# HGRN2 linear attention with a bilinear feed-forward layer: the states' part of a unit moved to the next unit's state sums, and the first two units rearranged

## The chip, the cores and the metric

The kernel runs on one core of a Trainium2 chip. The metric is the device time of one execution in microseconds; for each kernel several executions are timed and their median is given. A profile is one further execution, recorded by the hardware profiler. In it PE is the engine of the matrix products, DVE and ACT the two engines that work on whole tiles (vector and scalar engine), POOL the third of that kind, and SP the engine that here only issues DMAs.

## What is computed

Attention with a decaying state, for 4 batches, 8 heads, 768 tokens and 48 channels a head, and then a bilinear feed-forward layer on 3072 tokens of 384 channels, with 1536 inner channels. All inputs of the attention are fp32; the three weight matrices come as fp64.

```python
def _attn_ref(q, k, v, f_logit):
    f = 1.0 / (1.0 + np.exp(-f_logit))
    state = np.zeros((B, H, D, D), dtype=np.float32)
    for t in range(S):
        state = f[:, :, t, :, None] * state + np.einsum('bhd,bhe->bhde', k[:, :, t], v[:, :, t])
        y[:, :, t] = np.einsum('bhd,bhde->bhe', q[:, :, t], state)

def _moe_ref(x, w_a, w_b, w_out):
    a = x @ w_a
    b = x @ w_b
    return (a * b @ w_out).astype(np.float32)

# x is y with heads and channels of a token side by side: (B, H, S, D) -> (B*S, H*D)
```

## The kernel before

**Tiling.** `by_quotients` (L79) cuts the attention into 16 units. A unit `u` is one batch, one half of the sequence (`BLK` = 384 tokens) and four of the eight heads; two units after each other give all heads of one half, and so one block of 384 tokens of the feed-forward layer's input, `xT[blk]`, of which there are 8. Four heads lie in a tile of 128 partitions as two pairs: 48 rows of a head at partition 0, 48 of the next at partition 64, and the pairs side by side in the free dimension (`n`). `FIRST` are the units 0 and 1.

**The steps of a unit.** The decay's running products are divided into k and multiplied into q, and then everything is matrix products on 64-token pieces (`SUB`), of which a unit has 6 along the tokens:

- `load_unit` (L134) issues a unit's loads on SP. There are three sets of input tiles, so unit `u + 3` takes the place of unit `u`.
- `front` (L254), in four parts: sigmoids on ACT (L261 to L264), a scale on POOL (L266); scans on DVE (L271) and the test of whether the decay fits (`held`, L272); reciprocal and scans on DVE (L276, L281); products q and k (L283, L284).
- `scores` (L311): q times k on PE (L319), masked by DVE into `at` (L335).
- `turn` (L339): k transposed on PE (L347, products of 128 rows), copied into `kT` by ACT (L349, L351).
- `gains` (L355): what each piece adds to the state, kT times v on PE (L367, 24 products, 64 rows by 48 columns); then DVE adds these up along the tokens into `st`, one copy (L381) and five additions (L383), and scales the last for the next half (L390).
- `within` (L392): `at` times v (L401), into the PSUM banks of y.
- `across` (L410): state times q (L422), added into the same banks. Three copies, or four where two spare banks are used, bring y to SBUF (L435, into one tile `y` of a pool with one buffer; for the first two units ACT does those of the one bank and DVE those of the other), five small DMAs put its rows into `xT` (L450; for the first two units three on ACT's queue and two on SP's, later all on SP's), and then unit `u + 3` is loaded.

L319, L367, L401 and L422 are products on 64-row parts of PE's array: four of them, on the four quadrants, run side by side. All others use 128 rows. The profile has two records for each fp32 `matmul` of the code, so the 24 products of `gains` show as x48.

**The feed-forward layer.** `up` (L463) makes one 128-channel column of `x @ w_b` and of `x @ w_a` (L469, 12 records), `product` (L478) multiplies both (ACT copy L484, DVE L486). That is done so for the first two blocks, while the weights come in. The later blocks take `up_pair` (L528) with fewer, combined products, and `down` (L593) makes the output for two groups of 128 tokens. The weights come in pieces of 384 or 768 KB: `load_weights` (L175) issues the next piece on SP, and `from_double` (L191) makes fp32 of it in three parts, two on ACT (L202, L204, with a POOL operation; L207, L209) and one on DVE (L214, L216). `begin(n)` (L219) and `end(n)` (L230) run the first two parts and the last part of all pieces up to `n`; from the third piece on, two of them excepted, `end` also issues the load of a further piece.

**The order.** The program's order is written by hand (`tc.manual_schedule`). Each engine works through its own list in that order, and waits for the others by semaphores. Up to `up(0, 4)` the calls stand one by one (L701 to L801). From there a loop walks over `up`, `up_pair` and `down`, and between their parts `beside()` takes parts of units from a queue with due times. A unit's parts there are those of the generator `slot` (L652):

```python
def slot(u):
    nxt = front(u + 1) if u + 1 < NU else iter(())
    next(nxt, None)
    yield
    if u > 2 * NQ:
        within(u - 1)
    if u < NU:
        scores(u)
    next(nxt, None)
    yield
    if u < NU:
        turn(u)
    if u > 2 * NQ:
        across(u - 1)
    yield
    if u < NU:
        gains(u)
```

So the slot of unit `u` runs, in its second part, `within` of the unit before and `scores` of its own, in its third `turn` and `across` of the unit before, in its fourth `gains`. Between two parts stand products of the feed-forward layer, or none where both have the same due time.

## Time and profile before

| | us |
|---|---|
| median of 14 runs | 630.1 (628.55 to 631.92) |
| the profiled execution | 629.11 |
| its span, first to last instruction | 627.4 |
| PE busy in it | 593.7 |
| DVE, ACT, POOL busy | 377.7, 221.9, 62.8 |

The mean clock granted to PE was 0.984 of full speed. The page's busy times are sums over the span; the span has two very different stretches, and its slices and windows show them. Up to about 45 us units 0 and 1 go through all their steps and the first weight pieces arrive: 43.65 MB of DMA traffic in the whole span, with 185 to 255 GB/s in the first seven of 40 slices. After that PE works on the feed-forward layer, with units 2 to 15 in between.

What the head looks like, step by step, from the timelines of PE, DVE and ACT (start in us):

| step | unit 0 | unit 1 |
|---|---|---|
| k landed | 13.09 | |
| scores (L319) | 15.55 | 23.84 |
| mask (L335) | 18.32 | 25.93 |
| within (L401) | 19.35 | 26.59 |
| gains (L367) | 20.63 | 28.12 |
| states on DVE (L381, L383) | 21.90 | 29.55 |
| across (L422) | 23.25 | 29.86 |
| first copy of y (L435) | 24.25 | 33.20 |
| first DMA into xT (L450) | 25.35 | 33.84 |
| first products of block 0 (L469) | 32.03 | |

### The profile page before, as it was taken

The numbers are of one execution on the slowest core, as the hardware profiler recorded it, in microseconds if no ns is written. First come the engines' busy times: TensorE is split into PE (matmuls) and PEld (weight loads), VectorE is DVE, ScalarE is ACT, GpSimd is POOL, SyncE is SP. The second block draws the span as 40 slices with busy tenths as digits, with TensorE's granted clock in tenths as the row PEclk, the third lists the DMA queues.
The fourth block names the chain that finished last, engine by engine and source line by source line (L and its number), as shares of the span: only waits on it lengthen the run. The fifth ranks groups of instructions, "written<-read, shape, count | busy, mean of one in ns | idle before, by whom it ended". The sixth has DMA issues, their size and how long they took to land.

```text
span 627.4 us, 13968 instructions
## 1 busy us (share of the span) xinstructions
PE 593.7 (95%) x5922; PEld 537.1 (86%) x5922; DVE 377.7 (60%) x748; ACT 221.9 (35%) x400; POOL 62.8 (10%) x58
## 2 busy tenths in 40 slices
PE   0869899999999999999999999999999999999996
PEld 0736555558998999999999999999999999999995
DVE  6877445797877567646675567647564344534541
ACT  6578499722332243224312242323311232022200
POOL 6234154410000000000000000000000000000000
PEclk9869999999999999999999999999999999999998
DMA  8786775000144304130404012040001000000000
GB/s 235 222 254 192 189 248 187 1 1 1 46 108 115 96 7 90 41 83 1 96 1 120 27 32 65 11 111 2 20 1 46 26 19 2 2 27 0 1 26 30
DMA packets 30343, 43.65 MB, mean 70 GB/s; under 512 B 3776, under 2 KB 24896, under 8 KB 30272
## 3 DMA queue, kind: packets, MB, share of 16 engines
q1 hardware_dynamic: 29984, 42.38, 24.8%
q8 instruction: 48, 0.79, 0.6%
q10 hardware_dynamic: 288, 0.30, 0.2%
q14 instruction: 23, 0.19, 0.1%
HBM read 33.23 MB, written 4.72 MB: 60 GB/s over the span
## 4 chain that ended last, share of the span: by engine, by line
PE 87%; DMA 5%; DVE 2%; SPq 2%; ACT 1%; issue 1%; ACTq 0%; DVEq 0%
PE ps_f L542 41%; PE ps_f L610 23%; PE ps_f L469 14%; DMA xT<-y 2%; PE ps_y L401 2%; PE ps_x L319 2%; PE ps_x L367 2%; PE ps_y L422 1%; PE ps_x L347 1%; DMA v_in<-in_v_dram 1%; SPq L154 1%; SPq L450 1%; DMA out_dram<-o 1%; DMA k_in<-in_k_dram 1%; DMA q_in<-in_q_dram 1%
## 5 line engine op out<-in xcount | busy, mean ns | idle before, releaser
L542 PE MATMUL ps_f<-xT,w_ba 128*128 128x192 f32 x864 | 155.4, 327 | 0.0
L547 DVE TENSOR_TENSOR groups<-ps_f,groups 128x384 f32<-128x384 f32 x144 | 80.1, 558 | 118.5 <-ACT groups L559 99.5
L542 PEld LDWEIGHTS ps_f<-xT,w_ba 128*128 128x128 f32 x864 | 142.3, 190 | 0.5
L469 PE MATMUL ps_f<-xT,w_ba 128*128 128x384 f32 x288 | 98.2, 501 | 5.7 <-DVE w_ba L216 4.2
L469 PEld LDWEIGHTS ps_f<-xT,w_ba 128*128 128x128 f32 x288 | 55.2, 194 | 46.1 <-DVE w_ba L216 5.8
L542 PE MATMUL ps_f<-b_sb,raw 128*128 128x192 f32 x432 | 82.0, 326 | 0.0
L542 PEld LDWEIGHTS ps_f<-b_sb,raw 128*128 128x128 f32 x432 | 72.2, 190 | 0.0
L550 ACT COPY groups<-ps_f 128x384 f32<-128x384 f32 x36 | 17.3, 480 | 109.3 <-PE ps_f L542 103.6
L610 PE MATMUL ps_f<-w_out,h 128*128 128x192 f32 x288 | 52.0, 330 | 0.6 <-DVE o L605 0.6
L610 PE MATMUL ps_f<-w_out,groups 128*128 128x192 f32 x288 | 50.9, 327 | 0.0
L610 PE MATMUL ps_f<-spare,h 128*128 128x192 f32 x288 | 49.6, 328 | 0.2 <-DVE h L605 0.2
L610 PEld LDWEIGHTS ps_f<-w_out,h 128*128 128x128 f32 x288 | 46.8, 190 | 1.6 <-DVE o L605 0.9
L610 PEld LDWEIGHTS ps_f<-w_out,groups 128*128 128x128 f32 x288 | 47.3, 190 | 0.1
L610 PEld LDWEIGHTS ps_f<-spare,h 128*128 128x128 f32 x288 | 46.8, 190 | 0.8 <-issue 0.5
L205 POOL TENSOR_SCALAR h<-h 128x768 f32<-128x768 f32 (+1 forms) x20 | 40.6, 2028 | 49.4 <-ACT h L202 47.5
L266 POOL TENSOR_SCALAR inv<-inv 128x768 f32<-128x768 f32 x14 | 13.5, 962 | 306.2 <-ACT inv L262 306.2
L605 DVE TENSOR_TENSOR o<-ps_f,u 128x192 f32<-128x192 f32 x36 | 12.8, 355 | 44.0 <-PE ps_f L610 40.7
L572 DVE TENSOR_TENSOR groups<-groups 128x384 f32<-128x384 f32 x72 | 36.6, 549 | 0.0
L559 ACT COPY groups<-ps_f 128x384 f32<-128x384 f32 x36 | 17.3, 480 | 52.6 <-PE ps_f L542 52.6
L542 PE MATMUL ps_f<-xT,raw 128*128 128x192 f32 x144 | 29.8, 330 | 0.0
L542 PE MATMUL ps_f<-b_sb,w_ba 128*128 128x192 f32 x144 | 29.3, 326 | 0.0
L319 PE MATMUL ps_x<-q_in,k_in 48*64 48x64 f32 x672 | 13.7, 226 | 16.3 <-DVE start L276 15.6
(113 smaller groups left out, 700.6 us busy)
## 6 DMA issues: line engine op xcount, KB each, us to landing
q_in<-in_q_dram SPq DMA_DIRECT2D x32, 144.0 KB, 4.1
k_in<-in_k_dram SPq DMA_DIRECT2D x32, 144.0 KB, 3.5
v_in<-in_v_dram SPq DMA_DIRECT2D x16, 288.0 KB, 5.0
raw<-in_moe_w_out_dram SPq DMA_DIRECT2D x6, 768.0 KB, 4.3
out_dram<-o SPq DMA_DIRECT2D x24, 192.0 KB, 1.9
f_in<-in_f_logit_dram SPq DMA_DIRECT2D x28, 144.0 KB, 3.0
xT<-y SPq DMA_DIRECT2D x46, 72.0 KB, 2.2
raw<-in_moe_w_b_dram SPq DMA_DIRECT2D x4, 768.0 KB, 7.1
```

The source lines that it names most:

```text
L205: nc.gpsimd.tensor_scalar(h, h, HI_MAX, None, ALU.min)
L266: nc.gpsimd.tensor_scalar(inv, inv, EXP_K, 1.0, ALU.mult, ALU.add)
L319: nc.tensor.matmul(ps[h][SUB * p:SUB * p + SUB, o:o + SUB], lhsT=kf[r, tokens(n, c, p)], rhs=qf[r, tokens(n, c, p)], start=True, stop=True,)
L367: nc.tensor.matmul(ps_x[R * h:R * h + D, p, (n * NC + c) * D:(n * NC + c) * D + D], lhsT=kT[r, n, c, R * h:R * h + D], rhs=t["v"][r, n, c, ...
L469: nc.tensor.matmul(ps[nm][:, 0:BLK], lhsT=w[:, kt, ft * 128:ft * 128 + 128], rhs=x[:, kt], start=kt == 0, stop=kt == NKT - 1,)
L542: nc.tensor.matmul(to[:, g], lhsT=w[:, g, j], rhs=x, start=start and g == 0, stop=True, skip_group_check=True)
L547: nc.vector.tensor_tensor(c[:, :, k, i], x, y, ALU.add)
L550: nc.scalar.copy(p1, x0)
L559: nc.scalar.copy(u3, x0)
L572: nc.vector.tensor_tensor(to[:, :, 2 * j + k], a[:, :, k], b[:, :, k], ALU.mult)
L605: nc.vector.tensor_tensor(to, x, y, op)
L610: nc.tensor.matmul(to, lhsT=x[:, i], rhs=w[:, i], start=first and i == 0, stop=i == HFT - 1, skip_group_check=True)
```

## The change

Three things are done at once.

1. In `slot` one `yield` moves up: `across(u - 1)` leaves the part of `turn(u)` and stands at the head of the part of `gains(u)`.
2. For units 0 and 1: `y` lies in a slice of `groups` of its own for each unit rather than in the pool's one tile; all five DMAs into `xT` go on ACT's queue; unit 0's copies of y are all on ACT; `gains` sums the state up inside PSUM, with 48 products instead of 24, then one ACT copy and three DVE operations in place of one copy and five additions; the test `held` and the scaling for the next half move out into `check` and `carry`, which are called later.
3. The calls of the head are put into another order: unit 0's loads stand ahead of unit 1's, the first three weight pieces ahead of k of unit 0, `across(0)` behind `scores(1)` and `turn(1)`, `end(4)` (which begins and ends the fourth weight piece) ahead of `across(1)`, `turn(2)` ahead of `within(2)`.

```diff
--- before.py
+++ after.py
@@ -251,6 +251,10 @@
     def halves(x):
         return x.rearrange("p n s -> p (n s)")
 
+    def check(u):
+
+        nc.vector.tensor_tensor(held[:, u], products_of_f[u][:, :, BLK - 1], least, ALU.is_ge)
+
     def front(u):
 
         t = sets[u % NSET]
@@ -269,7 +273,8 @@
         for n in range(2):
             c = slice(n * BLK, n * BLK + BLK)
             nc.vector.tensor_tensor_scan(F[:, c], F[:, c], none, math.exp(MIDDLE), ALU.mult, ALU.add)
-        nc.vector.tensor_tensor(held[:, u], products_of_f[u][:, :, BLK - 1], least, ALU.is_ge)
+        if u not in FIRST:
+            check(u)
         yield
 
         start = sb2.tile([128, 2, NC - 1], FP32, tag="start", name="start")
@@ -357,6 +362,7 @@
         _, half, _ = unit(u)
         t, kT = sets[u % NSET], live[u]["kT"]
         last = half == NH - 1
+        at_once = u in FIRST
         for n in range(2):
             for c in range(NC):
                 for p in range(2):
@@ -364,16 +370,26 @@
                         continue
                     for h in range(2):
                         r = slice(SUB * p, SUB * p + SUB)
-                        nc.tensor.matmul(
-                            ps_x[R * h:R * h + D, p, (n * NC + c) * D:(n * NC + c) * D + D],
-                            lhsT=kT[r, n, c, R * h:R * h + D],
-                            rhs=t["v"][r, n, c, h * D:h * D + D],
-                            start=True,
-                            stop=True,
-                        )
+                        for ci in range(0 if at_once else c, c + 1):
+                            nc.tensor.matmul(
+                                ps_x[R * h:R * h + D, p, (n * NC + c) * D:(n * NC + c) * D + D],
+                                lhsT=kT[r, n, ci, R * h:R * h + D],
+                                rhs=t["v"][r, n, ci, h * D:h * D + D],
+                                start=ci == 0 or not at_once,
+                                stop=ci == c,
+                            )
         st = sb3.tile([128, NJ, 2, D], FP32, tag="st", name="st")
         before = live[u - NQ]["st"][NJ] if half else None
         live[u]["st"] = [before] + [st[:, j] for j in range(NJ - 1 if last else NJ)]
+        if at_once:
+
+            sums = [ps_x[:, p, 0:2 * NC * D].rearrange("r (n c d) -> r c n d", n=2, c=NC) for p in range(2)]
+            even, odd = (st.rearrange("r (c p) n d -> r p c n d", p=2)[:, p] for p in range(2))
+            nc.scalar.copy(odd, sums[1])
+            nc.vector.tensor_copy(even[:, 0], sums[0][:, 0])
+            nc.vector.tensor_tensor(even[:, 1:], sums[0][:, 1:], odd[:, 0:NC - 1], ALU.add)
+            nc.vector.tensor_tensor(odd, sums[0], odd, ALU.add)
+            return
         for j in range(NJ - 1 if last else NJ):
             c, p = divmod(j, 2)
             new = ps_x[:, p, 0:2 * NC * D].rearrange("r (n c d) -> r n c d", n=2, c=NC)[:, :, c]
@@ -382,9 +398,14 @@
             else:
                 nc.vector.tensor_tensor(st[:, j], before, new, ALU.add)
             before = st[:, j]
-        before = live[u]["st"][-1]
-        if not last:
-
+        carry(u)
+
+    def carry(u):
+
+        if u in FIRST:
+            check(u)
+        if unit(u)[1] < NH - 1:
+            before = live[u]["st"][-1]
             for n in range(2):
                 end = products_of_f[u][:, n, BLK - 1:BLK]
                 nc.vector.tensor_scalar(before[:, n], before[:, n], end, math.exp(-MIDDLE), ALU.mult, ALU.mult)
@@ -427,11 +448,15 @@
                         stop=True,
                         skip_group_check=True,
                     )
-        y = sb1.tile([128, 2 * NC, 2, SUB], FP32, tag="y", name="y")
+        if u in FIRST:
+
+            y = groups[:, NTG, u * 2 * BLK:u * 2 * BLK + 2 * BLK].rearrange("r (o p m) -> r o p m", p=2, m=SUB)
+        else:
+            y = sb1.tile([128, 2 * NC, 2, SUB], FP32, tag="y", name="y")
 
         whole = [(0, 0, 0, 128)] if ps[0] is y_banks[0] else [(0, 0, 0, D), (0, R, R, D)]
         for p, e, r, rows in (*whole, (1, R, 0, D), (1, 0, R, D)):
-            copy = nc.vector.tensor_copy if u in FIRST and p else nc.scalar.copy
+            copy = nc.vector.tensor_copy if u == 1 and p else nc.scalar.copy
             copy(y[r:r + rows, :, p], ps[p][e:e + rows, 0:BLK].rearrange("r (o m) -> r o m", m=SUB))
         give_back(ps)
         y = y.rearrange("r (n c) p m -> r n (c p m)", n=2)
@@ -446,7 +471,7 @@
                     kt, p = divmod(ch, 128)
                     w = min(left, 128 - p)
 
-                    queue = nc.scalar if u < NQ and (n + h) % 2 else nc.sync
+                    queue = nc.scalar if u in FIRST else nc.sync
                     queue.dma_start(out=xT[blk][p:p + w, kt], in_=y[row:row + w, n])
                     ch, row, left = ch + w, row + w, left - w
         live.pop(u - NQ, None)
@@ -662,9 +687,9 @@
         yield
         if u < NU:
             turn(u)
+        yield
         if u > 2 * NQ:
             across(u - 1)
-        yield
         if u < NU:
             gains(u)
         yield
@@ -713,92 +738,93 @@
 
         load_unit(0, "f")
         load_unit(1, "f")
+        patterns()
+        load_weights()
+        load_weights()
+        next(fronts[0])
+        load_unit(0, "q")
+        load_weights()
+        next(fronts[1])
+        next(fronts[0])
+        load_unit(2, "f")
+        load_unit(0, "k")
+        next(fronts[1])
+        load_unit(0, "v")
         next(fronts[0])
         load_unit(1, "q")
-        load_unit(0, "q")
-        load_unit(1, "k")
-        load_weights()
-        load_unit(0, "k")
-        load_weights()
-        patterns()
         next(fronts[0])
-        load_weights()
-        next(fronts[0])
-        load_unit(1, "v")
-        next(fronts[1])
-        next(fronts[1])
-        next(fronts[0])
-        load_unit(0, "v")
         next(fronts[1])
         begin(3)
-        load_unit(2, "k")
-        load_unit(2, "f")
         scores(0)
-        load_unit(2, "v")
+        load_unit(1, "v")
+        turn(0, True)
+        load_unit(1, "k")
         next(fronts[1])
-        turn(0, True)
         within(0)
         gains(0)
+        next(fronts[2])
+        load_unit(2, "v")
+        scores(1, True)
+        load_weights()
+        turn(1, True)
+        load_unit(2, "k")
         load_unit(NSET, "f")
-        load_weights()
+        load_unit(NSET + 1, "k")
+        end(3)
+        load_unit(2, "q")
+        across(0)
         next(fronts[2])
-        turn(1, True)
-        across(0)
-        load_weights()
-        scores(1, True)
-        end(2)
         within(1, True)
-        load_unit(2, "q")
         gains(1)
+        end(4)
         across(1)
-        load_weights()
+        begin(4.5)
         next(fronts[2])
         next(fronts[3])
-        end(3)
-        next(fronts[2])
-
-
-        up(0, 0)
         next(fronts[2])
         load_unit(NSET, "q")
-        begin(4.5)
+
+
+        up(0, 0)
+        product()
+        load_unit(NSET + 1, "f")
+        load_unit(NSET, "v")
+        next(fronts[3])
+        carry(0)
+        scores(2, True)
+        up(0, 1)
+        begin(5)
+        end(6)
         load_weights()
         product()
-        load_unit(NSET, "v")
-        end(4)
-        scores(2, True)
-        up(0, 1)
-        next(fronts[3])
-        load_unit(NSET + 1, "q")
-        end(5)
-        load_unit(NSET, "k")
-        end(6)
+        turn(2, True)
         within(2)
-        load_unit(NSET + 1, "f")
-        load_unit(NSET + 1, "k")
-        turn(2, True)
         load_weights()
         gains(2)
-        load_unit(NSET + 1, "v")
+        up(0, 2)
+        load_unit(NSET, "k")
+        begin(7)
         next(fronts[3])
+        load_weights()
         next(fronts[3])
         product()
-        begin(7)
-        up(0, 2)
-        product()
         across(2)
+        begin(8)
         up(0, 3)
-        begin(8)
         scores(3)
         turn(3, True)
+        load_weights()
+        carry(1)
         within(3)
+        load_unit(NSET + 1, "q")
         gains(3)
         across(3)
-        up(0, 4)
         end(7)
         product()
+        load_unit(NSET + 1, "v")
+        up(0, 4)
+        end(8)
         product()
-        end(8)
```

## The prediction

> **What bounds the kernel now.** I read the page first, then a table of windows, PE's waits, the chain of waits, and last the timeline of PE around one unit.
>
> ```profile
> PE   0869899999999999999999999999999999999996
> PEclk9869999999999999999999999999999999999998
> ```
> ```profile
> 27.00:40.50 13.50, 7.96 (x138) 5.19 (x139) 10.68 (x25) 5.06 (x8) 2.44 (x2) 0.50 0.70 206
> 74.00:624.00 550.00, 545.56 (x5097) 504.59 (x5095) 325.46 (x642) 176.67 (x331) 35.53 (x24) 1.00 0.19 50
> ```
>
> The columns of the windows are stretch, its length, busy time and count of PE, weight load, DVE, ACT, POOL, then granted clock, DMA share and GB/s. From 74 to 624 us PE is busy for 545.56 of 550 us at full clock: there the time is the length of PE's own list of products, and only what shortens this list counts. Before that PE waits, and at 27 to 40.5 us its clock is 0.50, so the head is a chain of other engines' work:
>
> ```profile
> PE ps_x L319 <- DVE start L276: 15.6, 1, 15.6
> PE ps_f L469 <- DVE w_ba L216: 4.2, 1, 4.2
> ```
> ```profile
> 27.27 5.83 DMA xT<-y
> ...
> 35.64 4.72 DMA xT<-y
> ...
> 40.50 4.49 PE ps_f L469 x8
> ```
> ```profile
> 33.20 0.97 ACT L435 COPY y<-ps_f 48x384 f32<-48x384 f32 x2 [8.46 <-DMA xT<-y]
> ```
>
> The chain goes: y of unit 0 copied, its last small DMA into xT lands at 27.27 + 5.83 = 33.10; the one y buffer comes free, y of unit 1 is copied at 33.2 (ACT had stood idle for 8.46 us before this copy), its DMAs go out until 35.64, the last lands 4.72 us later, and the first block's products go on at 40.50. Two parts are thus to be judged: PE's list after 74 us, and the moment that stands at 40.50 here.
>
> **What the Trainium skill says.** "TensorEngine Tiling (Array Packing)", section Tiling Modes, under Key Properties: a change of the tiling mode, not of the tile alone, drains the TensorE, while tiles of one mode run independently. The trace agrees, and gives the price:
>
> ```profile
> 287.57 2.11 PE L542 MATMUL ps_f<-xT,w_ba 128*128 128x192 f32 x12
> 289.61 0.89 PE L401 MATMUL ps_y<-at,v_in 64*48 64x64 f32 x48
> 290.32 0.92 PE L319 MATMUL ps_x<-q_in,k_in 48*64 48x64 f32 x48
> 291.16 1.57 PE L542 MATMUL ps_f<-xT,w_ba 128*128 128x192 f32 x8
> ...
> 295.17 0.81 PE L542 MATMUL ps_f<-b_sb,raw 128*128 128x192 f32 x4
> 295.82 0.82 PE L347 MATMUL ps_x<-ident,k_in 128*128 128x128 f32 x6
> 296.56 0.87 PE L422 MATMUL ps_y<-q_in,st 48*48 48x64 f32 x40
> 297.37 0.92 PE L542 MATMUL ps_f<-xT,raw 128*128 128x192 f32 x4
> 298.12 2.11 PE L542 MATMUL ps_f<-xT,w_ba 128*128 128x192 f32 x12
> 300.17 0.74 PE L367 MATMUL ps_x<-v_in,kT 64*48 64x48 f32 x40
> 300.84 1.57 PE L542 MATMUL ps_f<-xT,w_ba 128*128 128x192 f32 x8
> 302.24 1.46 PE L542 MATMUL ps_f<-b_sb,raw 128*128 128x192 f32 x8
> ```
>
> Durations overlap in the pipeline, so I read differences of starts. Four full products take 0.65 us (295.17 to 295.82). Twelve should take 1.95 and take 2.05 up to the gains (298.12 to 300.17): going in costs 0.10. The eight after it take 1.40 instead of 1.30, the four after across 0.75 instead of 0.65: coming out costs 0.10. "DMA: Bandwidth & Descriptors", section "Issuing engines are not separate DMA queues": queues of several engines share the same DMA engines, so another issuer saves only its own issue time. The 4.72 and 5.83 us agree: both stood behind a 768 KB weight load that SP had issued. "TensorE: Matmul & The Clock Gate", Part 1: half rate after idling, in a window of about 3.4 us; agrees with 0.50 at 27 to 40.5 us, the clock coming back only within the next 4.5 us (mean 0.62).
>
> **Part 1: across moved from the turn to the gains.** The arithmetic is unchanged. In the new order of PE's instructions, across stands immediately ahead of gains in the 8 slots where it stood apart before: slot 5 and slots 9 to 15. In slots 6 to 8 turn, across and gains already lay next to each other, slot 4 has no across, the last no gains. In each of the 8, one way in and one way out go: 2 x 0.10 = 0.20 us by the starts above. Each batch of 64-row products also fills and empties for itself. By the single starts in the trace, its first four passes take 60 to 74 ns where later fours take 25 to 36, and from its last product to the first full one it is 135 to 146 ns, while from within to scores it is 36. That is 0.03 + 0.10, so about 0.34 us a unit, against 0.20 if these ends overlap something. I take 8 x 0.34 = **2.7 us** gained (bounds 1.6 and 2.9).
>
> What could eat it: across now comes one step later, so y, its copies (L435 on ACT), SP's xT DMAs and the next load_unit come a step later, about 3 us. Those queued behind them on SP are the loads of a unit three ahead, needed five or more steps later, and the xT of a block that has further units to wait for. The gains come no later than before, but stand behind across; their 6 adds on DVE (0.28 us each) feed the next unit's states, half a dozen steps off. The transposes are now followed at once by full products, whose inputs are old. PE is ahead of nothing here, so I cost it at nothing; if an xT came late it would cost at most the step, 3 us, once a block.
>
> **Part 2: sums at once, y tiles, queues, new head order.** From the durations above and the head's timeline:
> - Reordered loads: ahead of k of unit 0 now stand f of two units, two 384 KB weight pieces, q of unit 0, a 768 KB piece and f of unit 2, instead of 2.1 MB of f, q, k and one piece. f ended at 6.86 us; with 1.1 us for 384 KB, 1.2 for a q, k or f of a unit, 2.05 for 768 KB: 6.86 + 2.2 + 1.2 + 2.05 + 1.2 + 1.2 = 14.7, against 13.09. DVE's scans had the scores wait until 15.55, so they come at about 15.9: +0.3. The gains then start near 21.0 (before: 20.63).
> - The gains of units 0 and 1 issue 48 products each instead of 24. 24 took 1.15 us at half clock (20.63 to 21.78). Doubled: 2.0 to 2.3. On DVE one copy and five adds (0.26 + 1.40) become an ACT copy of 288 (0.4) and DVE operations of 96, 192 and 288 (about 1.1 together): 1.5 against 1.66, nearly even. Sums of unit 0 are ready near 24.8 (23.6 before), and across(0) stands behind scores(1) and turn(1), ending near 25.95 (24.2 before).
> - ACT does all three copies of y(0), behind the sigmoids of unit 2 (2.0) and the kT copies of unit 1: 26.55 to 28.0. Then it issues all five DMAs itself, 0.61 each: to 31.1. Behind these waits ACT's copy of the sums of unit 1, at 31.1; with DVE's part across(1) runs 32.0 to 34.2 (before 29.87 to 32.1).
> - Then the conversion of the fourth weight piece (`end(4)`: four ACT operations, 3.55 us with overlap) is queued ahead of the copies of y(1): 31.6 to 35.1, copies to 36.1 on ACT and, behind DVE's L214 and L216, to 37.4 on DVE. There is no wait for a buffer any more; before, these copies ran at 33.2 to 34.4. So the 8.46 us of waiting were worth only 33.2 - 32.1 = 1.1 us, and ACT's queue takes more than that back.
> - Five issues, 36.9 to 39.4, the last landing in 1.9 to 2.5 us, as no 768 KB load is ahead of it now: about 41.5. Before: 40.37.
> The moment at 40.50 goes to about 41.6: +1.1. Two switches go in the head too (within(2) now follows turn(2)), and the weight pieces come in another order, none on the path by my reckoning. Kept on to the third unit, whose xT landed at 73.09, I take **+1.3 us** for the head (bounds -0.5, where the copies of y(1) slip in front, to +5).
>
> **Sum.** -2.7 + 1.3 = -1.4 us, against the profiled execution: span 627.4, with what lies around it 629.11, to 627.7. The median of the runs, 630.1, lies 1.0 above that execution; the same difference gives **628.7 us**. A comparison of this kernel tells 0.2%, 1.26 us, from no change.
>
> **Rivals.**
> - B, slower: ACT's queue becomes the end of the head. Two groups of five issues, a copy, a conversion and y(1) stand in one line on ACT. For it: 2.12 us for three issues in the line of 25.98 us (0.71 each; single ones up to 0.83), and nothing on ACT can overtake. Against it: ACT was only 5.06 of 13.5 us busy there. Price: ten issues at 0.83 give +2.2, and one more 3.4 us window at half clock loses 1.7; 1.3 + 2.2 + 1.7 = +5.2 in the head, -2.7 after: 632.6. It decides if the DMAs of y(1) go out after 40 us.
> - C, faster: the head is neutral. The free y tile and the 3 us that DMAs no longer lose behind 768 KB loads cancel the ACT queue: 630.1 - 2.7 = 627.4; with a head 0.5 to 1.5 earlier, 626 to 627. For it: both xT waits of the chain, 5.83 and 4.72. Against it: the times worked out above.
> - D, the merging gains little: fewer crossings, but across and gains side by side wait for the four quadrants or for kT (L349, which has 0.3 and 0.2 us in PE's waits). It saves 0 to 1: with the head's 1.3, 630.4 to 631.4.
>
> **How the numbers follow.** A 0.45, B 0.20, C 0.23, D 0.12. A spreads over 627.2 to 630.2: 0.26 of it faster than the bound, 0.19 within. C: 0.20 and 0.03. B: 0.18 slower, 0.02 within. D: 0.06 within, 0.06 slower. Together faster 0.46, same 0.30, slower 0.24. The range 626.0 to 631.8 leaves out most of B (0.14) and the end of C (0.05). A alone: 627.2 to 630.2.
>
> **What would show it.** In the timeline of PE after 74 us: L422 followed directly by L367 and one late start instead of two; the stretch from there to the end shorter by 2 to 3 us. In the head: the scores of unit 0 at 15.9, no long wait ahead of L435, the last xT of unit 1 landing at 41 to 42, PE busy without gaps from a start about 1 us later. I am wrong if the products of the first block go on before 40.3 or after 43.5, or if full products after the turn wait.

## The result

| | median us | runs | ratio to before (95% interval) |
|---|---|---|---|
| before | 630.07 | 47 (628.36 to 631.92) | 1 |
| changed | 637.12 | 10 (635.16 to 641.02) | 1.0111 (1.0098 to 1.0124) |

The changed kernel is slower by 7.0 us; 628.7 was predicted, in a range of 626.0 to 631.8. Its profiled execution took 634.15 us with a span of 632.4, which is 3 us under its median, so the profile shows 5.0 of the 7 us, and what follows from it gives places rather than exact sizes.

### The profile after

First the page and the windows that answer to those of before (columns as there). From 74 us on PE is idle for 7.1 us where it was 4.4; the 2.7 us between have the length of one wait, shown below. In the head the clock of 0.81 from 27 to 40.5 us is no gain: it is 0.50 from 40.5 to 45, where it was 0.62 before.

```profile
PE   0659799999999999999999999999999999999996
PEclk9969989999999999999999999999999999999998
```
```profile
27.00:40.50 13.50, 7.52 (x237) 5.63 (x232) 9.95 (x20) 7.01 (x12) 2.13 (x1) 0.81 0.80 228
74.00:629.00 555.00, 547.87 (x5106) 506.42 (x5104) 327.17 (x645) 176.04 (x331) 35.06 (x24) 1.00 0.19 52
```

PE's waits in the changed kernel (what waits, for whom; us in total, times, longest):

```profile
PE ps_f L494 <- DMA xT<-groups: 4.5, 2, 3.9
PE ps_f L324 <- issue: 2.8, 1, 2.8
PE ps_f L494 <- DMA xT<-y: 2.7, 1, 2.7
PE ps_f L443 <- DVE st L389: 2.6, 1, 2.6
```

L494 is `up`, L324 `scores`, L443 `across`. Before's list has for `up` 4.2 us for a converted weight piece (shown above) and

```profile
PE ps_f L469 <- DMA xT<-y: 1.5, 2, 0.9
PE ps_f L401 <- issue: 1.7, 1, 1.7
```

of which 0.9 stand ahead of 40.50 and the other 0.5 ahead of 73.23; for the first state that `across` takes it waits 0.4. And the chain of waits, before (first two lines; block 0 is shown above) and after:

```profile
70.89 2.20 DMA xT<-y
73.23 72.59 PE ps_f L469 x224
```
```profile
42.09 2.19 DMA xT<-groups
...
44.38 5.07 PE ps_f L494 x8
...
72.16 6.10 DMA xT<-y
...
78.55 11.61 PE ps_f L494 x30
```

Before, the first block went on at 40.50; now it is 44.38. So 3.9 us are lost up to unit 1's transfer, and 3.7 of them are still there at across of unit 3 (69.93 against 66.19). Block 1 goes on at 78.55 where it was 73.23, after a wait of 2.7 us where it was 0.5: 2.2 us more. This wait is paid twice, since PE's clock falls after it; 4 us at a mean of 0.58 lose 1.7 us:

```profile
79.00:83.00 4.00, 4.00 (x9) 2.22 (x8) 0.00 (x0) 2.58 (x4) 1.23 (x1) 0.58 1.07 222
```

At the scores of unit 4 the changed kernel is thus 7.5 us late (153.30 against 145.75). A third, smaller loss follows there: from these scores to `within` of unit 4 it takes 17.16 us where it took 16.25, and in it PE waits for the `product` ahead (L511) once:

```profile
PE ps_f L635 <- DVE groups L511: 0.7, 1, 0.7
```

Against this stands the gain of the moved yield. The lag is +8.5 us at `within` of unit 4 (170.46 against 162.00), and then it shrinks slot by slot: at `within` of units 8, 9, 10, 11 and 15 it is +8.1, +7.7, +7.4, +6.2 and +4.8. So 3.7, 3.8 and 0.9 us are lost in three places and 3.6 gained, which leaves 4.8 of the 5.0 that the spans differ by. The slot of unit 10 in the PE timeline of the changed kernel shows how:

```profile
304.87 2.11 PE L567 MATMUL ps_f<-xT,w_ba 128*128 128x192 f32 x12
306.91 0.71 PE L443 MATMUL ps_y<-q_in,st 48*48 48x64 f32 x34
...
307.60 0.72 PE L374 MATMUL ps_x<-v_in,kT 64*48 64x48 f32 x36
308.25 1.57 PE L567 MATMUL ps_f<-xT,w_ba 128*128 128x192 f32 x8
```

Across (L443) and gains (L374) run into each other, with one way in and one way out.

### The profile page after: what moved, and what is told of

Same layout as the page of the kernel before. It is cut to its first block, busy times and chain, and to the rows that moved or that the text cites. A ratio compares the mean times of both kernels' runs of the same rounds, so it can differ in the third digit from the quotient of the medians.

```text
span 632.4 us, 14154 instructions
## 1 busy us (share of the span) xinstructions
PE 592.2 (94%) x6018; PEld 537.1 (85%) x6018; DVE 374.1 (59%) x740; ACT 223.1 (35%) x404; POOL 62.5 (10%) x58
## 4 chain that ended last, share of the span: by engine, by line
PE 87%; issue 4%; DMA 2%; DVE 2%; ACT 2%; POOL 1%; SPq 1%; ACTq 0%; DVEq 0%; POOLq 0%
PE ps_f L567 41%; PE ps_f L635 25%; PE ps_f L494 14%; PE ps_y L422 2%; PE ps_x L324 1%; PE ps_x L374 1%; PE ps_y L443 1%; POOL h L205 1%; PE ps_x L352 1%; DMA xT<-y 1%; DMA k_in<-in_k_dram 1%; DMA f_in<-in_f_logit_dram 1%; SPq L475 0%; DVE h L630 0%; ACT kT L356 0%
## 5 line engine op out<-in xcount | busy, mean ns | idle before, releaser
L494 PE MATMUL ps_f<-xT,w_ba 128*128 128x384 f32 x288 | 100.3, 509 | 7.2 <-DMA xT<-groups 4.5
L494 PEld LDWEIGHTS ps_f<-xT,w_ba 128*128 128x128 f32 x288 | 56.2, 198 | 48.6 <-DMA xT<-groups 6.7
L324 PE MATMUL ps_x<-q_in,k_in 48*64 48x64 f32 x672 | 13.7, 226 | 17.8 <-DMA q_in<-in_q_dram 17.1
```

The lines of the kernel that those rows point to most:

```text
L324: nc.tensor.matmul(ps[h][SUB * p:SUB * p + SUB, o:o + SUB], lhsT=kf[r, tokens(n, c, p)], rhs=qf[r, tokens(n, c, p)], start=True, stop=True,)
L494: nc.tensor.matmul(ps[nm][:, 0:BLK], lhsT=w[:, kt, ft * 128:ft * 128 + 128], rhs=x[:, kt], start=kt == 0, stop=kt == NKT - 1,)
```

## The experiments

Eighteen further kernels were run, each timed beside the kernel before. I name the parts of the change: S the moved yield, Y the y tiles of their own, Q ACT's queue and copies, G the sums at once, O the new order of the head. Ratios are to the kernel before of the same group of runs. The other nine come further down.

| run | parts | median us | ratio (95% interval) |
|---|---|---|---|
| e1_slot_only | S | 627.08 | 0.9956 (0.9941 to 0.9972) |
| e8_slot_and_y | S Y | 624.98 | 0.9930 (0.9912 to 0.9947) |
| e11_y_and_queue | S Y Q | 627.80 | 0.9965 (0.9953 to 0.9978) |
| e10_y_and_sums | S Y G | 628.62 | 0.9981 (0.9970 to 0.9993) |
| e3_old_order | S Y Q G | 630.74 | 1.0018 (1.0005 to 1.0030) |
| e12_order_alone | S Y O | 634.47 | 1.0072 (1.0055 to 1.0090) |
| e5_old_sums | S Y Q O | 632.02 | 1.0041 (1.0026 to 1.0057) |
| e4_split_queues | S Y G O, copies of Q | 635.61 | 1.0096 (1.0075 to 1.0118) |
| changed kernel | S Y Q G O | 637.12 | 1.0111 (1.0098 to 1.0124) |
| e2_head_only | Y Q G O | 638.20 | 1.0140 (1.0117 to 1.0164) |

### Which part costs

**e1: the yield alone.**
```diff
 # the kernel before
-        if u > 2 * NQ:
-            across(u - 1)
         yield
+        if u > 2 * NQ:
+            across(u - 1)
         if u < NU:
             gains(u)
```


> The kernel before with the one yield moved and nothing else. Theory M (merging saves about 0.34 us in each of 8 slots, the head costs the rest): 2.7 to 3.6 us faster than before, so about 627 us. Rival N (merging saves nothing, waits take its place): within 0.7 us of before, 630. Unit by unit in the trace, M expects the lead over before to grow by 0.3 to 0.4 us a slot from slot 9 to slot 15.

It is 2.8 us faster (0.44% of 630), with an interval of 1.8 to 3.7, so M holds. In the eight slots that lost a crossing the lead grows by 0.32 to 0.34 us each, but for one: between `within` of unit 10 and that of unit 11 it grows by 1.23. There the chain of the kernel before had something else on it:

```profile
338.82 4.37 DMA out_dram<-o
...
343.32 0.37 DVE o L605
```

SP had issued seven loads of unit 13 ahead of an output DMA; DVE's write into o waited for this output, and PE 0.6 us for DVE. With across one step later the loads stand behind the output, and in this stretch PE waits for nobody. All eight slots together give 3.6 us in this trace, 0.9 more than the crossings.

**e2: everything but the yield.**
```diff
 # the changed kernel
-        yield
         if u > 2 * NQ:
             across(u - 1)
+        yield
         if u < NU:
             gains(u)
```


> The changed kernel with the yield put back, so that only the first two units and the order of the head differ from before. M: 2.7 to 3.6 us slower than the changed kernel, about 640 us, 10 above before. N: as the changed kernel, 637. The first products of block 1 should then start about 5 us later than before, as in the changed kernel.

8.8 us slower than before, 1.8 us more than the changed kernel: the sign of M, at a smaller size than forecast and than e1 gives. This difference is known to 1.7 us only, so the two agree within their intervals. In the trace the lag stays at 8.40 to 8.62 us from `within` of unit 4 to the end, where that of the changed kernel shrinks: from there on only the yield's gain is left, and everything else has been lost ahead of it.

**e3 and e4: the old order, and split queues.**
```diff
 # e3: the changed kernel, with the head's calls of before, and
         gains(0)
+        carry(0)
...
         gains(1)
+        carry(1)
```


> The changed kernel with the head's calls in the order of before (scaling for the next half right after each of the first two state sums); y tiles of their own, five DMAs on ACT's queue, sums at once and the moved yield stay. Theory O (the order is what costs: loads and conversions queue behind it, and the transfers into xT of unit 3 fall behind weight loads): nearly all of the head's loss goes, 626 to 629 us. Rival Q (the five DMAs on ACT's queue cost it) and rival G (the doubled sums cost it): 633 to 637, since both are still there.


```diff
 # e4: the changed kernel
-                    queue = nc.scalar if u in FIRST else nc.sync
+                    queue = nc.scalar if u < NQ and (n + h) % 2 else nc.sync
```


> The changed kernel with the DMAs of the first two units split over ACT and SP as before (two on SP, or three), all else as changed. Rival Q (ACT's five issues, 3.97 us for unit 0 in the trace, hold up ACT's copy of unit 1's sums): 3 to 5 us faster than the changed kernel, 632 to 634. Theory O: within 1.5 us of it, 635.5 to 638.5, since SP's queue then has the wait instead.

The old order takes back 6 of the 7 us, but at 630.7 lies above what O gave: Y, Q and G together still cost something. Splitting the queues brings about 1 us, within O's band. So the order is the largest part, and the queue not the one that I had feared.

**e5, e8, e10, e11, e12: the parts one by one.** The edit of each is the part itself, put on or taken off:
```diff
 # e5: the changed kernel
-        at_once = u in FIRST
+        at_once = False
...
-        carry(0)
-        carry(1)
```


> The changed kernel with the state sums of units 0 and 1 as before: 24 products each, one copy and five additions on DVE, scaling and test right after them; order, queues and y tiles as changed. Theory G (48 products more a unit make PE fetch its instructions earlier and more often; in the changed kernel PE stood 2.79 us in the scores of unit 1 and 0.70 in its gains with no engine to wait for, while a 16,384 byte packet of the instruction queue was under way; and ACT's copy of the sums stands behind the five DMA issues): 2 to 3.5 us faster than the changed kernel, 633.5 to 635. Theory O (order alone): within 1 us of 637.


```diff
 # e8: e1
-        y = sb1.tile([128, 2 * NC, 2, SUB], FP32, tag="y", name="y")
+        if u in FIRST:
+            y = groups[:, NTG, u * 2 * BLK:u * 2 * BLK + 2 * BLK].rearrange("r (o p m) -> r o p m", p=2, m=SUB)
+        else:
+            y = sb1.tile([128, 2 * NC, 2, SUB], FP32, tag="y", name="y")
```


> The kernel before with the moved yield and with y of units 0 and 1 in tiles of their own; queues, sums and order as before. If the wait of unit 1's copies for the buffer was worth the 1.1 us of my prediction: 1 us faster than the yield alone, 626.1. If the transfer that ends the head stands behind a weight piece anyway: 627, no difference.


```diff
 # e10: e3
-            copy = nc.vector.tensor_copy if u == 1 and p else nc.scalar.copy
+            copy = nc.vector.tensor_copy if u in FIRST and p else nc.scalar.copy
...
-                    queue = nc.scalar if u in FIRST else nc.sync
+                    queue = nc.scalar if u < NQ and (n + h) % 2 else nc.sync
```


> The kernel with the moved yield and y tiles of their own (624.98), with the state sums of the first two units at once added, in the old order and with the old queues. Theory G (doubled products cost PE's instruction supply and put ACT's copy on the path): 3 to 5 us slower than without, 628 to 630. Rival (they cost only in the new order): 624.5 to 626.


```diff
 # e11: e8
-            copy = nc.vector.tensor_copy if u in FIRST and p else nc.scalar.copy
+            copy = nc.vector.tensor_copy if u == 1 and p else nc.scalar.copy
...
-                    queue = nc.scalar if u < NQ and (n + h) % 2 else nc.sync
+                    queue = nc.scalar if u in FIRST else nc.sync
```


> The kernel with the moved yield and y tiles of their own (624.98), with all five DMAs of the first two units on ACT's queue and unit 0's copies of y on ACT added, in the old order and with the old sums. Theory Q (ten issues and three copies in one line on ACT hold up the sigmoids, conversions and y of unit 1): 1.5 to 3 us slower, 626.5 to 628. Rival: within 0.7 us of 625, as SP is free for the loads in that time.


```diff
 # e12: e5, with copies and queues as before
-            copy = nc.vector.tensor_copy if u == 1 and p else nc.scalar.copy
+            copy = nc.vector.tensor_copy if u in FIRST and p else nc.scalar.copy
...
-                    queue = nc.scalar if u in FIRST else nc.sync
+                    queue = nc.scalar if u < NQ and (n + h) % 2 else nc.sync
```


> The kernel with the moved yield and y tiles of their own (624.98), in the new order of the head, but with the old sums and the old queues. Theory O (the order costs by itself: k of unit 0 2.7 us later, loads stopped at f of units 3 and 4, xT of unit 3 behind a weight piece): 5 to 7 us slower, 630 to 632. Rival (the order costs only together with the sums at once and ACT's queue): 625 to 628.

With ratios times 630 us, one after the other: S -2.8; Y -1.6 (e8 to e1); O +8.9 (e12 to e8); Q on top of it -2.0 (e5 to e12); G on top of these +4.4 (the changed kernel to e5). Each is known to 1.0 to 1.6 us; that they sum up to the whole +7.0 is so by the way they are taken. In the old order the same parts cost otherwise: Q +2.2 (e11 to e8), G +3.2 (e10 to e8), both +5.5 (e3 to e8), so there they add up. Theory O holds (e12 came out above its 630 to 632), theory G too (e5 gained more than its 2 to 3.5), and theory Q in the old order. Q turns its sign from there to the new order with the old sums; with the sums at once the queue seems to cost about 1 us there (e4, known to 1.6). Its price is not a property of the edit.

What G costs shows in PE's timeline of e8 and e10, which differ in G alone. Gains and across of unit 1 in e8, the old sums:

```profile
27.28 0.71 PE L367 MATMUL ps_x<-v_in,kT 64*48 64x48 f32 x46
28.47 1.80 PE L422 MATMUL ps_f<-q_in,st 48*48 48x64 f32 x40 [0.47 <-DVE st L381]
```

and in e10, the sums at once:

```profile
30.48 2.88 PE L374 MATMUL ps_x<-v_in,kT 64*48 64x48 f32 x94
34.13 0.32 PE L443 MATMUL ps_f<-q_in,st 48*48 48x64 f32 x4 [0.78 <-DVE st L389]
```

The doubled products last 2.88 us here, at a lower clock (0.54 from 30 to 33.4 us), against 0.71. From the end of gains to the end of across it is about the same, 2.3 us, in both: the additions saved on DVE bring nothing, because in the old form across starts on the first sum while DVE makes the others. Unit 1's across then ends 5.4 us later, and the first block goes on 5.1 later (43.14 against 38.08). Of the 3 us by which its gains begin late, about 1.5 are the doubled gains of unit 0, and 0.8 a wait for v of unit 0, which landed later in e10.

### What in the new order costs

**e6, e7, e9: one cause at a time.**
```diff
 # e6: the changed kernel
         gains(1)
-        end(4)
         across(1)
+        end(4)
         begin(4.5)
```


> The changed kernel with the conversion of the fourth weight piece behind across of unit 1 instead of ahead of it. If the line on ACT and POOL ahead of the copies of unit 1's y sets the end of the head (my step: copies at 37.7 to 40.1, although across ended at 36.6), then the copies start at about 36.7 and the first block goes on 2 to 3 us earlier: 634 to 635. Rival (DMA order decides): the gain is lost again at the transfer of unit 3 or at the weight piece itself, 636 to 638.


```diff
 # e7: the changed kernel
-        load_unit(NSET + 1, "f")
         load_unit(NSET, "v")
...
         product()
+        load_unit(NSET + 1, "f")
         across(2)
```


> The changed kernel with one load moved: f of unit 4 (which waits for POOL's memset, and this for ACT and POOL) leaves its place ahead of the loads of v, k and three weight pieces on SP's queue and goes behind them, ahead of across of unit 2. Theory W (SP stands from 41.7 to 47.5 us at that load, so the weight pieces come some 10 us later than before, and the transfers into xT of unit 3 share the DMA engines with a 768 KB piece; PE waits 2.7 us for them and then runs 3.4 us at half clock): PE's wait for xT of unit 3 goes, 3 to 4.5 us faster, 632.5 to 634. Rival (it is lost before unit 3): within 1 us of 637.


```diff
 # e9: the changed kernel
         turn(3, True)
-        load_weights()
         carry(1)
         within(3)
-        load_unit(NSET + 1, "q")
         gains(3)
         across(3)
+        load_weights()
+        load_unit(NSET + 1, "q")
```


> The changed kernel with one weight piece (768 KB) and q of unit 4 issued behind across of unit 3 instead of ahead of it; nothing else. Theory W2 (the transfers into xT of unit 3, landed at 78.3 to 79.0 us, stand behind these two loads; moving one f load left them there and gained nothing): PE's wait for xT of unit 3 falls from 2.7 to under 1 us and the half clock after it goes, 3 to 4.5 us faster, 633 to 634. Rival (weight pieces are late then, and PE waits for them in block 1): within 1.5 us of 637.

636.47, 637.55 and 637.70 us (ratios 1.0101, 1.0122, 1.0120): none of them gains more than 0.6. In e6 the first block goes on earlier, but the scores of unit 2 wait 1.6 us for the moved conversion instead. In e7 SP no longer stands at the f load and issues the weight pieces from 42.8 us on, but the transfers of unit 3 still stand behind a later piece, and PE's wait for them, which was to go, is 4.3 us. In e9 these transfers land at 76.9, and PE's wait for them is 0.6; but then

```profile
90.82 1.65 PE L494 MATMUL ps_f<-xT,w_ba 128*128 128x384 f32 x2 [3.25 <-ACT b_sb L509]
```
```profile
86.82 0.89 ACT L202 ACTIVATE h<-raw 128x768 f32<-128x768 f32 x1 [4.81 <-DMA raw<-in_moe_w_a_dram]
```

The second line is ACT's in e9: it stood 4.81 us in front of the conversion of the moved piece, with the copies that give PE its PSUM banks (L509) queued behind it. So one shortage is passed round. SP's issues in the changed kernel show where it begins:

```profile
47.87 0.79 SPq L154 DMA_DIRECT2D f_in<-in_f_logit_dram  x2
...
69.50 0.46 SPq L188 DMA_DIRECT2D raw<-in_moe_w_a_dram  x1
...
72.16 3.40 SPq L475 DMA_DIRECT2D xT<-y  x5
```

SP issues nothing from 38.8 to 47.9 us, since f of unit 4 waits for POOL's memset, which stands behind a conversion and the sigmoids of unit 3 on POOL and ACT. The kernel before stands at an f load as well, from 43.7 to 49.8, but it had issued three weight pieces ahead of it (at 35.9, 37.8 and 38.9). Here they come behind it, and the fourth at 69.50, just ahead of xT of unit 3. Summing the issues with those into xT, 12.7 MB had been asked for by 66 us, before it were 15.2; 1.2 MB of the difference are the four loads behind unit 2's transfers, which begin at 61.75 there and at 66.05 here.

**e13: the stream of loads mended in whole.**
```diff
 # the changed kernel
-        load_unit(NSET + 1, "f")
         load_unit(NSET, "v")
...
         next(fronts[3])
         load_weights()
+        load_weights()
         next(fronts[3])
         product()
+        load_unit(NSET + 1, "f")
         across(2)
...
         turn(3, True)
-        load_weights()
         carry(1)
         within(3)
-        load_unit(NSET + 1, "q")
         gains(3)
         across(3)
+        load_unit(NSET + 1, "q")
```


> The changed kernel with four loads moved: f of unit 4 behind the weight pieces (as in the run with f later), the fourth of those pieces next to the third instead of ahead of xT of unit 3, and q of unit 4 behind across of unit 3. Theory W3 (the two runs before each mended one half: with f later xT of unit 3 still stood behind a piece, with loads behind PE got xT in time but waited 3.2 us for the late piece at 90.7; both halves are one delay of the stream of loads, some 1.7 MB behind at 66 us): both waits are gone, 3.5 to 5 us faster than the changed kernel, 632 to 633.5. Rival (a further wait takes their place): 636 to 638.

633.60 us, ratio 1.0059 (1.0040 to 1.0078): 3.3 us gained by the ratio and 3.5 by the medians, at the lower end of W3's band of 3.5 to 5. The wait for unit 3 is

```profile
PE ps_f L494 <- DMA xT<-y: 0.9, 1, 0.9
```

and no wait of PE for a weight piece follows it. Both waits are gone together, as W3 has it, at a size slightly under the one forecast.

**e14, e15, e17: DVE's line ahead of unit 1's states.** In e12, the order alone, DVE's timeline ahead of unit 1's sums (L397) reads

```profile
27.62 0.96 DVE L216 CUSTOM_DVE_ANT_0 w_ba<-h,spare 128x1536 uint16<-128x1536 uint16 x1
28.61 1.14 DVE L460 COPY groups<-ps_y 48x384 f32<-48x384 f32 x2
29.79 1.80 DVE L275 TENSOR_TENSOR_SCAN f_in<-f_in,zero 128x384 f32<-128x384 f32 x2
31.62 0.16 DVE L256 TENSOR_TENSOR held<-f_in,least 128x2 f32<-128x2 f32 x1
31.70 0.25 DVE L397 COPY st<-ps_x 128x96 f32<-128x96 f32 x1
```

while PE waits 3.3 us for them. The edits:
```diff
 # e14: e12
         across(0)
-        next(fronts[2])
         within(1, True)
         gains(1)
-        end(4)
         across(1)
+        next(fronts[2])
+        end(4)
         begin(4.5)
```


> The run with the order alone (634.47) with unit 2's scan on DVE and the conversion of the fourth piece behind across of unit 1. Theory D (in that run DVE had conversions, copies of y and this scan, 25.0 to 31.6 us, ahead of unit 1's state sums, and PE waited 3.3 us for them): across of unit 1 starts about 29.9 instead of 32.0, 1.5 to 2.5 us faster, 632 to 633. Rival (the transfers decide): within 0.7 us of 634.5.

e15 is e12 with the edits of e13 (without `carry`, which e12 hasn't there) and of e14.

> The order alone with both: the four loads moved and scan and conversion behind across of unit 1. If W3 and D are the order's costs and add: 4 and 2 us, 628 to 629 us, which leaves some 3.5 us of the order's 9 for k of unit 0 coming 2.7 us later and the rest. If one hides the other: 630 to 632.


```diff
 # e17: e15, DVE's part of three conversions moved, their load left
-        end(3)
+        load_weights()
         load_unit(2, "q")
         across(0)
         within(1, True)
         gains(1)
         across(1)
+        for i in range(3):
+            next(going[i], None)
+        ended[0] = 3
         next(fronts[2])
```


> The run with both (630.13) with DVE's part of the first three weight conversions behind across of unit 1 too; the loads stay where they are. In the run with the scan behind, DVE still had 3.6 us of conversions (26.9 to 30.5) and the copies of y of unit 0 ahead of unit 1's sums. If this is what is left of the order's price: across of unit 1 starts 2 us earlier, 627.5 to 628.5. If the transfers or the later conversions decide: 629.5 to 631.

e14: 633.89 (1.0064), 0.5 us gained, so D fails at that size: unit 1's sums started at 31.7 as in e12. Its whole head had begun 1.0 us later in that execution, the conversions and copies of y were still ahead of the sums, the scores of unit 2 then waited 2.2 us for the scan that had been moved, and the wait for unit 3's transfer was still 2.8. e15: 630.13 (1.0001, 0.9988 to 1.0015): 4.5 us gained, at the edge of the case in which one hides the other (630 to 632). Its sums of unit 1 start at 29.64, 2.1 us earlier than in e12. e17: 628.56 (0.9978, 0.9963 to 0.9992): 1.4 us more, known to 1.3 us, and at the edge of its first case; but its sums start at 29.36, 0.3 earlier than in e15 (in an execution whose head began 0.7 later) and not the 2 forecast, so where it gains is not shown. Of O's 8.9 us, 4.5 are thus the loads with the scan (e13 and e14 suggest mostly the loads; they were not moved alone in e12), 1.4 the conversions, and 3.0 (0.9978 to 0.9930) are left.

For 0.9 of these 3.0 the traces show a place. From the scores to `within` of unit 4 it is 16.24 to 16.25 us in all eight traces in the old order and 17.16 to 17.17 in all twelve in the new one, each of these with the wait of 0.7 us for L511 that the changed kernel shows. Why the order brings this wait was not tried. The other 2.1 stay open. Two things would fit: k of unit 0 comes late, its scores starting at 17 instead of 15.5 us, and e17, which moved the scan of unit 2, has a wait for it that e12 has not:

```profile
PE ps_f L324 <- DVE k_in L289: 2.7, 1, 2.7
```

The second would be a price of the mending, not of O. Neither was tried by itself.

### The fastest

```diff
 # e16: e8
         across(1)
-        load_weights()
...
         up(0, 0)
+        load_weights()
```


> The kernel with the moved yield and y tiles of their own (624.98) in the old order, with the 768 KB weight piece that SP issued between the two DMAs of unit 1 into xT and the last one moved behind the first products of block 0. If this piece holds up the last transfer (chain of before: 4.72 us), 1 to 2 us faster, 623 to 624. If the piece itself is then late: 625 to 627.


```diff
 # e18: e8
         across(1)
         load_weights()
+        end(3)
         next(fronts[2])
         next(fronts[3])
-        end(3)
         next(fronts[2])
```


> The kernel with the moved yield and y tiles of their own (624.98) with the last part of the third weight piece's conversion ahead of unit 2's scan on DVE, as PE waited 3.2 us for it at 35.3. If this wait is on the path: up to 1.5 us faster, 623.5 to 624.5. If unit 1's transfers (products go on at 38.1) end the head anyway: 624.5 to 625.5.

625.79 (0.9932, 0.9915 to 0.9949) and 625.61 (0.9936, 0.9916 to 0.9955): no gain over e8. Moving the piece in front of the last transfer or the third piece's conversion does not end e8's head earlier; in e16 the moved piece may have taken its gain back, as the second case of its expectation has it. What ends this head was not found. So e8, two parts of the five, is the fastest kernel of the study, with e16 and e18 no different within their intervals: 624.98 us, 0.9930 of before, and 12 us under the changed kernel.

## Why the prediction was wrong

- **Part 1 was right.** 2.7 us were predicted, -2.8 measured for the yield alone, with 0.32 to 0.34 a slot against 0.34. That nothing is lost by across coming later held. What I said of SP's queue, that the loads behind it have time, was true; that it also frees an output DMA once, worth 0.9 us in e1's trace, was not seen. So the mechanism and the price of a slot are right, and that the total of 2.8 falls so near to 2.7 is in part luck.
- **Part 2 was wrong: +1.3 predicted, +8.8 to +9.8 measured** (e2 by itself, or 7.0 + 2.8). Its sum failed in four terms, and its own sign of being wrong came true: the first block went on after 43.5, at 44.38.
 - The sentence "the weight pieces come in another order, none on the path by my reckoning", and with it that the shift at 40.50 is only "kept on to the third unit". I had followed the moved loads up to xT of unit 1 and stopped. Between 38.8 and 47.9 us SP stands in front of one f load, and the delay comes out 25 us later, at xT of unit 3 or at a late piece, with the half clock behind it. e13 puts this at 3.3 us; the trace has 2.2 us of wait and 1.7 of clock.
 - The sums at once, "1.5 against 1.66, nearly even". The figure for DVE was right and so was the duration of the doubled products (1.83 us for 93 of 96 records, at 21.47; 2.0 to 2.3 predicted). Mis-sized was what it replaces: I priced DVE's five additions as if across had to wait for all of them, but it begins after the first. And PE's stop in the scores of unit 1, 2.79 us, was not in the sum (before there is one of 1.7 ahead of `within` of unit 1). G measures +3.2 to +4.4, where I had 0.85 to 1.15 a unit on PE and nearly nothing on DVE.
 - The head's start, ACT's line and DVE's. k of unit 0 was to land at 14.7 and its scores to start at 15.9; DVE's product of k waited for it until 15.91, and the scores started at 17.08. The five issues on ACT were to end at 31.1:

```profile
15.91 0.96 DVE L289 TENSOR_TENSOR k_in<-k_in,inv 128x768 f32<-128x768 f32 x1 [1.66 <-DMA k_in<-in_k_dram]
```
```profile
31.20 1.80 DVE L275 TENSOR_TENSOR_SCAN f_in<-f_in,zero 128x384 f32<-128x384 f32 x2
33.04 0.16 DVE L256 TENSOR_TENSOR held<-f_in,least 128x2 f32<-128x2 f32 x1
```
```profile
29.77 3.97 ACTq L475 DMA_DIRECT2D xT<-groups  x5
33.83 0.40 ACT L388 COPY st<-ps_x 128x288 f32<-128x288 f32 x1 [3.60 <-DVE held L256]
```

 They began 1.8 us later than forecast, 1.2 of it from k, and took 0.79 each instead of 0.61. Had ACT been free at 31.1, DVE would not have been: the conversions of three weight pieces and unit 2's scan, which the prediction has not ahead of these sums, kept it until 33.2. That fits e4, where the split queues bring only 1 us. All steps behind them (copy of the sums, across of unit 1, conversion, copies of y) came in the predicted sequence and 2.3 to 2.8 us late, and the first block went on 3.9 us later than before instead of 1.1. ACT's sequence was right, its start was late.
 - PE's wait for L511 at unit 4, 0.9 us with what follows from it, was not in the sum either.
- **The buffer wait.** I called the 8.46 us in front of unit 1's copies worth 1.1. Y alone gives 1.6, known to 1.5: the sign is right, the size can't be told from it.
- **The clock.** The prediction says that its trace agrees with a clock that falls after idling, in a window of 3.4 us. The rate of 0.50 fits, and so does the size (4 us at a mean of 0.58 are 3.4 at half and the rest at full); but in the kernel before, PE's longest stop between its first product at 15.55 and the fall at about 27 us is 1.7 us (with the clock still at 0.99 from 20 to 27), and the fall at 79 us in the changed kernel follows 2.7 us. Here waits shorter than that window were enough.
- **Rival B** named a slower result through ACT's queue, at 632.6. The direction came true and its sign of it too: unit 1's DMAs went out from 39.6 to 42.1. But its mechanism was not the main one, for in the new order without the doubled sums the same queue and copies are a gain of 2.0 us (e5 against e12). The case that came about, loads that fall behind as a whole, was not among the rivals.

## What to carry to other kernels

Merging two batches of 64-row products is worth its two crossings, and a price read off two neighbouring starts in the timeline held here in the sum over eight slots. An order of loads has to be followed to the end of the stream, not to the first block that gets its data: find the instruction at which the issuing queue stands, and add up the bytes issued by a later time in both orders. If a mended wait comes back elsewhere at about the same size, as in e9, look for a shortage ahead of both places. And a rewritten stretch with several edits is best tried part by part: here two of the five gain 4.4 us, and the others hid it.

## What was not expected of the hardware

PE stopped in the middle of a batch of products, with no engine to wait for. In the changed kernel, the scores of unit 1:

```profile
26.46 0.62 PE L324 MATMUL ps_f<-q_in,k_in 48*64 48x64 f32 x26 [2.79 <-issue]
```

The page lists an instruction queue with 49 packets and 0.80 MB in all; in the trace one packet of 16,384 bytes is under way from 23.81 us for 1.32 us, just after PE stopped at 23.7. Such a stop, of 0.7 to 2.8 us, comes after 220 recorded products in all twelve traces in the new order: in the scores of unit 1 where the sums are at once, in across of unit 0 where they are not (e5, e12, e14, e15 and e17). After 348, which is 128 more, it comes in e3 and e11 (2.5 and 2.4 us) and, shorter (0.4 to 1.0 us), as a second stop in the changed kernel, e2, e4, e6, e9 and e13. So inside a batch the place goes by the count of instructions and not by what they do. That points to PE running out of fetched instructions: 128 products with their 128 weight loads would fill one such packet at 64 bytes each, an estimate from the packet's size, and the kernels with doubled sums have 49 packets where all others have 48. Products of 64 rows use instructions up fast: 93 of them took 1.83 us in the changed kernel's gains of unit 0, while twelve of 128x384 took 4.14.

The other traces in the old order stop at neither count. There a stop of 1.4 to 2.2 us stands between scores and `within` of unit 1, after 244 products, in e10 after 292. The kernel before makes the mask for this `within` from 25.93 us on and goes on at 26.59, so this one is more likely a wait for DVE, though the view calls it issue. The cause of the stops inside a batch is read from the coincidence; no run took it apart from the rest.
